# Convolution by short transforms: the last tile's slots 13-16 turned on TensorE and copied inside SBUF

## The chip, the cores and the metric

The kernel runs on one core of a Trainium2 chip. The metric is the device time in microseconds of one execution. Five engines with a queue of their own work side by side: PE (TensorE, matrix products; its weight loads are listed as PEld), DVE (VectorE), ACT (ScalarE), POOL (GpSimd) and SP (SyncE, which only issues transfers here). Each runs its instructions in the order in which they were written and waits where one of them needs something. Transfers are issued by SP or by ACT and moved by 16 DMA engines that both share. A row of the profile with SPq or ACTq is the issue of a transfer, not the transfer itself.

## The reference

```python
# x: (1, 224, 224, 96), w: (7, 7, 96, 96), both bf16
wp = jnp.pad(w, ((0, H - K), (0, W - K), (0, 0), (0, 0)))
Xf = rfft2(x, axes=(1, 2)); Wf = rfft2(wp, axes=(0, 1))      # in f32
Yf = jnp.einsum('bhwi,hwio->bhwo', Xf, Wf)
y = irfft2(Yf, s=(H, W), axes=(1, 2)).astype(jnp.bfloat16)
```

That is a circular 7x7 convolution of a 224 by 224 image with 96 channels in and 96 out.

## The kernel before

The image's 224 rows are cut into NJ = 8 blocks of B = 28 rows, and each block, with 6 rows of overlap, is taken through a short transform along the height. It has NS = 17 **slots**, each a pair of real numbers (real and imaginary part; slots 0 and 16 hold two real points each). Along the width the 7 taps are applied directly, on even and odd pixels apart. The width is cut into NT = 7 **tiles** of 32 pixels; the last is TL = 6.

A tile goes through three stages.

1. Into slots (`a_jobs`, `f_jobs`): products of image rows (tile `xn`) with the transform matrix `Fm` give `xf`, the tile's spectrum, with 96 channels on the partitions.
2. The slots (`b_round`, one call per slot). `jit` makes planes `J` of sums and differences of `xf` on DVE, for three slots at a time. Then, in PE's order: the first group of tap products into the PSUM bank `b0`, whatever `mid()` puts in, and the second group (14 products) into `b1`. ACT scales part of `b0` by -0.5 (`SE.mul`, rows `tt__NNNN<-pb`), DVE makes `u` and `v` from it (in the last tile these lie in the free `xn` buffers, so the rows say `xn<-...`), and the slot's result `yf = v + u` is summed by POOL (`ysum(GE)`) or DVE (`ysum(VE)`). In the last tile DVE takes it where `s % 3 == 2` or `s >= 14`, POOL otherwise. Where planes are made in the same round, POOL's sum waits for the last of them.
3. Back to rows (`c_jobs`). `yf` has (pixel pair, row block) on its 128 partitions; the way back needs (row block, slot, part) there. That turn goes through scratch in HBM: groups of slots are put out (`put`, `scr`, `scra`, `scrb`) and read back in the other order (`load_t`, into `tt`). Products with the matrix `G` (rows `pb<-tt,Gm`) give rows of the image, which are evicted to `yo` or `J` and written to `out`.

For tiles 0 to 5, stage 3 runs late, as filler between the slots of a later tile: `fills` and `pace` give each round of `b_round` its jobs, in `mid()` and in `end()`. Six jobs of tile 5 are left when the slots of tile 6 are done; they run behind them (`cj.pop(0)()`), and their output puts are held in `outs` until all jobs are issued.

`_Ordered` makes each engine follow the order in which its instructions are written. `evac` gives each PSUM eviction to DVE or ACT by a running sum of costs (`load`), and `tail_evac` does so behind the slots.

The last tile has no later slots to hide its way back. Its slots are split by `SLAST` = (0, 9, 12, 15, 17):

- Slots 0-8 are put to `scra` and read back by one load of 864 KB into `tl_a`, in slot 11 (`SLOAD[0]`). The products with `GA` (`first`) take these.
- Slots 9-11 and 12-14 are put to `scrb` and read back by `load_b`, into `tl_b`: the first in slot 14, the second behind the slots, on SP behind the turned copies.
- Slots 15 and 16 are turned on chip (`turn`): a product with the permutation `PT`, an eviction to `zt`, and two copies of 48 KB from SBUF to SBUF into `tl_b`, each to 8 partitions, issued on SP.

All of `tl_a` and `tl_b` lies in one `xf` buffer that is free by then (rows `xf<-scra`, `xf<-scrb`, `xf<-zt`). The products with `GB` (`second`) close the sums of `first`, wait for everything in `tl_b`, and are followed by the last evictions and eight output puts (`out_dram<-tt`). Between `first` and `second` stand WARM = 8 products without use, so that PE isn't idle.

The puts of the last tile are issued on ACT, one round late: `puts.append` in the round of a group's last slot, `puts.pop` in the next round, just behind its `SE.mul`. `YGRPL` says which slots are put together: always three, up to slots 12-14.

```python
if s in plan: ...                       # planes of the next slots: at s = 0, 3, 6, 9, 12
ydve = bool(now) if t < TL else s % 3 == 2 or s >= NS - 3
```

Of the kernel before, what the change touches and what calls it, by code (L numbers as in the profile page):

```python
# [32 lines left out]
NSLOT = 2 + 3 * (NS - 1)  # L33
PGRP = ((0, 5), (5, 8), (8, 11), (11, 14), (14, 17))
YGRP = ((0, 3), (3, 6), (6, 9), (9, 12), (12, 15), (15, 17))
YGRPL = ((0, 3), (3, 6), (6, 9), (9, 12), (12, 15), (15, 17))
SLAST = (0, 9, 12, 15, 17)
SA = SLAST[1]
ND = SLAST[-2]
SLOAD = (SA + 2, 14)  # L40
YMAX = 3
YBUF = 4
JGB = ((0, 3), (3, 6), (6, 9), (9, 12), (12, 15), (15, 17))
# [4 lines left out]
SH3 = (0, 8, 17)  # L48
MERGE = ()
NP2 = 0  # L50
WARM = 8
HEAD = ("w",) * 6 + ("x0", "w", "w", "h0", "h1", "w", "w", "x1", "w", "w")
W1 = 30
ZC = 48
# [12 lines left out]
def kernel(  # L67
# [50 lines left out]
    def bank():  # L118
        return pools["psb"].tile([128, 512], F32, name="pb")
# [30 lines left out]
    def dma(out_ap, in_ap):  # L150
        return DE.dma_start(out=out_ap, in_=in_ap)
# [455 lines left out]
    def b_round(t, s, mid, end, ydve=False, planes=()):  # L607
# [90 lines left out]
        if t == TL and s >= ND:  # L698
            turns[s] = yv.rearrange("p r m o -> p (r m o)")
        elif s == y1 - 1:  # L700
            dst, yo0 = scr_tiles[t], 0
            if t == TL:
                i = sum(s >= v for v in SLAST[1:])
                dst, yo0 = scr_tiles[(t, i)], SLAST[i]

            def put(eng=DE):
                eng.dma_start(out=dst.rearrange("w j s e -> (w j) s e")[:, y0 - yo0:y1 - yo0],
                              in_=yf[:, 0:y1 - y0].rearrange("p s r m o -> p s (r m o)"))
            if t == TL:
                puts.append(lambda: put(SE))  # L710
            else:
                put()
# [2 lines left out]
    tt_tiles = {}  # L715
    puts = []
    turns = {}

    def turn(s, copy):
        pz, i = bank()[:, 0:4 * C], s - ND  # L720
        TE.matmul(pz, lhsT=PT[:], rhs=turns[s], start=True, stop=True)
        copy(out=zt[i][:], in_=pz)
        n = 2 * (NS - ND)
        for r in range(2):
            p = RB[-1] + 2 * i + r
            dma(tl_b[p:p + (NJ - 1) * n + 1:n].rearrange("p w e -> p (w e)"), zt[i][:, r * 2 * C:(r + 1) * 2 * C])

    def load_t(t, gi, h):
        tt = t2_pool.tile([128, 12, 2 * C], BF16, name="tt2") if gi == 2 else t_pool.tile([128, 8, 2 * C], BF16, name="tt")
# [39 lines left out]
    def c_jobs(t):  # L769
        jobs = []  # L770
        w0 = t * 2 * TW
        for gi, h in LT if t < TL - 1 else LTL:
            hold = {}
            nq = 2 if gi < 2 else 3

            def mk_(q, gi=gi, h=h, nq=nq, hold=hold):
                def put(j0, nj, px, npx, row, col):
                    yo = hold["yo"]

                    def go():  # L780
                        dma(out[0, j0 * B:(j0 + nj) * B, w0 + px:w0 + px + npx, :].rearrange("h w c -> h (w c)"),
                            yo[row:row + nj * B, col:col + npx * C])
                    if tail[0] or t == TL - 1 and gi != 2:
                        outs.append(go)
                    else:
                        go()

                def f():
                    if q % 2 == 0:
                        hold["yo"] = new_yo()  # L790
                    tt = tt_tiles[(t, gi, h)]
                    yo = hold["yo"]
                    nj = 2 if q == 2 else 3
                    for b in range(2):
                        pb = bank()[0:nj * B, 0:4 * C]
                        TE.matmul(pb, lhsT=G[0:nj * FR, 0:nj * B],
                                  rhs=tt[0:nj * FR, 4 * q + 2 * b:4 * q + 2 * b + 2, :].rearrange("p w e -> p (w e)"), start=True, stop=True)
                        k = 2 * (q % 2) + b
                        evac(yo[0:nj * B, k * 4 * C:(k + 1) * 4 * C], pb, 4 * C)
                    if q == 1 and gi < 2:  # L800
                        put(gi * 3, 3, h * PXC, PXC, 0, 0)
                    elif q == 1:
                        put(6, 2, 0, 16, 0, 0)
                        for j in range(2):
                            put(6 + j, 1, 24, 8, 2 * B, j * 8 * C)
                    elif q == 2:
                        put(6, 2, 16, 8, 0, 0)
                    if q == nq - 1:
                        held[gi == 2] -= 1
                        pump()  # L810
                return f
            for q in range(nq):
                jobs.append(mk_(q))
        return jobs

    LT = ((0, 0), (1, 0), (2, 0), (0, 1), (1, 1))
    LTL = ((2, 0), (0, 0), (1, 0), (0, 1), (1, 1))
    outs = []
    NTT = 4
    held = [0, 0]  # L820
    pend = []
# [67 lines left out]
    for r in range(NS + LAG):  # L889
        if r == 0:  # L890
            for i in range(1, PGRP[0][1]):
                add(max(2 * i - 3, 0), 2 * i - 1, [diff(i)])
            for i in range(N5, REAL[1]):
                add(2 * i - (3 if i % 3 == 0 else 2), 2 * i - (i % 3 == 0), [diff(i)])
            add(0, 4, fj[1][0] + fj[1][1])
            add(8, 12, fj[2][0] + fj[2][1])
        if r == 2:
            new_xf(1, SH2[0], SH2[1])
        for p in range(3):
            if r == (1, 3, 6)[p]:  # L900
                if p:
                    new_xf(1, SH2[p], SH2[p + 1])
                else:
                    xf_tiles[1] = xf_bufs[1]
                fj = f_jobs(1, p)
                if p == 2:
                    for jg in range(2):
                        fj[jg][-1] = then_load(fj[jg][-1], 2, jg)
                add((4, 7, 12)[p], (7, 11, 15)[p], fj[0] + fj[1])
        for p in range(2):  # L910
            if r == SH3[p + 1] + 1 - p:
                new_xf(2, SH3[p], SH3[p + 1])
                fj = f_jobs(2, p)
                if p:
                    for jg in range(2):
                        fj[jg][-1] = then_load(fj[jg][-1], 3, jg)
                add(2 * r, 2 * r + (12, 5)[p], fj[0] + fj[1])
        if r == PGRP[-2][1] + 1:
            assert not any(q[2] for q in qs[:len(PGRP) - 1])
            wtmp_cm.__exit__(None, None, None)  # L920
            t_pool = ctx.enter_context(tc.tile_pool(name="tt", bufs=NTT, side="right"))
            t2_pool = ctx.enter_context(tc.tile_pool(name="tt2", bufs=1, side="right"))
            yo_pool = ctx.enter_context(tc.tile_pool(name="yo", bufs=2, side="right"))
            g_pool = ctx.enter_context(tc.tile_pool(name="gp", bufs=1, side="right"))
            GA = g_pool.tile([KA, 4 * B], BF16, name="GA")
            GB = g_pool.tile([128, 2, 4 * B], BF16, name="GB")
            GE.memset(GA[:], 0.0)
            GE.memset(GB[:], 0.0)
            PT = g_pool.tile([128, 128], BF16, name="PT")
            zt = [g_pool.tile([128, 4 * C], BF16, name=f"zt{i}") for i in range(NS - ND)]  # L930
            GE.memset(PT[:], 0.0)
            pv = PT.rearrange("p (j w) -> p j w", j=NJ)
            GE.affine_select(out=pv, in_=pv, pattern=[[-1, NJ], [-NJ, TW]], compare_op=ALU.not_equal, fill=1.0, base=0, channel_multiplier=1)
        if r == 3:
            g_fin()
        for t in range(2):
            s = r - LAG * t
            if not 0 <= s < NS:
                continue
            now = bursts.pop((r, t), ())  # L940
            now = jit(*now) if now else []
            now, rest = rest + now[:2], now[2:]
            both = LAG <= r < NS
            b_round(t, s, fills(qs, 2 * r + (t if both else 0)), fills(qs, 2 * r + (t if both else 1)), False, now)
            if r == 0:
                for d in load_x(1, 1):
                    tc.add_manual_dep(d.ins, held_x.ins.name, SYNC, reason="second half behind the first products")
# [8 lines left out]
    for t in range(2, NT):  # L956
# [22 lines left out]
        for s in range(NS):  # L979
# [10 lines left out]
            if t == TL and s in SLOAD:  # L990
                i = SLOAD.index(s)
                if i:
                    load_b(i - 1)
                else:
                    dma(tl_a.rearrange("p w g e -> p (w g) e"),
                        scr_tiles[(TL, 0)].rearrange("w (g j) s (r e) -> (j s r) (w g) e", g=2, r=2))
            b_round(t, s, fills(qs, 2 * s), fills(qs, 2 * s + 1), bool(now) if t < TL else s % 3 == 2 or s >= NS - 3, now)
    tail[0] = 1
    load["v"], load["a"] = 1000.0, 0.0
    turn(NS - 2, SE.copy)  # L1000
    for _ in range(2):
        cj.pop(0)()
    turn(NS - 1, VE.tensor_copy)
    load_b(NL - 3)
    while cj:
        cj.pop(0)()
    assert not pend
# [65 lines left out]
```

## Time and profile before

| | |
|---|---|
| runs | 263.37 us median of 3 (263.31 to 264.7) |
| profiled execution | 263.98 us; first to last instruction 262.3 us |
| PE busy | 250.6 us of the span |
| last product of slot 16 | 243.9 us |
| slot 16's sum ready | 245.16 us |
| closing products begin | 252.16 us |
| last eviction ends | 258.85 us |

Nearly every row has line L101, because all operations are recorded in the helper `_Ordered`. Rows are told apart by what they write and read: `pb` is a PSUM bank, `WF` the transformed weights, `xf`, `J`, `yf`, `zt`, `tt`, `yo` as above. Times are in microseconds from the first instruction. In a timeline, the columns are start, length, engine, line, operation, what it writes and reads, and in square brackets the idle time of the engine before it with what ended it.

### The profile page before, as it was taken

The numbers are of one execution on the slowest core, as the hardware profiler recorded it, in microseconds if no ns is written. First come the engines' busy times: TensorE is split into PE (matmuls) and PEld (weight loads), VectorE is DVE, ScalarE is ACT, GpSimd is POOL, SyncE is SP. The second block draws the span as 40 slices with busy tenths as digits, with TensorE's granted clock in tenths as the row PEclk, the third lists the DMA queues.
The fourth block names the chain that finished last, engine by engine and source line by source line (L and its number), as shares of the span: only waits on it lengthen the run. The fifth ranks groups of instructions, "written<-read, shape, count | busy, mean of one in ns | idle before, by whom it ended". The sixth has DMA issues, their size and how long they took to land.

```text
span 262.3 us, 11952 instructions
## 1 busy us (share of the span) xinstructions
PE 250.6 (96%) x5038; PEld 231.7 (88%) x5038; DVE 220.9 (84%) x463; ACT 197.4 (75%) x471; POOL 98.7 (38%) x154
## 2 busy tenths in 40 slices
PE   8999999999999999999999999999999999999873
PEld 3879999999989999989999998999999989979642
DVE  6889998899999879877887788878989799999833
ACT  8879968697745967988988789897988853564522
POOL 7782233464657532232223322334123422325000
PEclk9999999999999999999999999999999999999987
DMA  7995104511111698987985495949949942788984
GB/s 182 268 185 134 47 6 143 169 51 47 47 49 50 189 267 145 322 251 195 265 232 190 139 280 165 229 115 300 278 164 214 296 143 82 201 215 223 201 272 151
DMA packets 46766, 46.58 MB, mean 178 GB/s; under 512 B 35312, under 2 KB 37940, under 8 KB 46712
## 3 DMA queue, kind: packets, MB, share of 16 engines
q1 hardware_dynamic: 45992, 44.34, 61.4%
q10 hardware_dynamic: 720, 1.47, 1.7%
q8 instruction: 39, 0.64, 1.0%
q14 instruction: 15, 0.12, 0.2%
HBM read 24.46 MB, written 21.14 MB: 174 GB/s over the span
## 4 chain that ended last, share of the span: by engine, by line
PE 68%; DVE 12%; DMA 9%; issue 4%; ACT 3%; POOL 2%; SPq 1%; DVEq 0%; POOLq 0%; ACTq 0%
PE pb L101 66%; DVE J L101 4%; DMA tt<-scr 3%; DMA WF<-in_x_dram 3%; DVE xn L101 2%; DVE WF L101 2%; DVE yf L101 2%; DMA wq<-in_w_dram 2%; POOL yf L101 2%; SPq L101 1%; DMA xf<-scrb 1%; ACT xf L101 1%; DVE v L101 1%; PE ps L101 1%; ACT WF L101 1%
## 5 line engine op out<-in xcount | busy, mean ns | idle before, releaser
L101 PE MATMUL pb<-WF,J 96*128 96x96 bf16 x2821 | 162.4, 206 | 1.6 <-DVE J L101 0.8
L101 PEld LDWEIGHTS <-J 96*128 96x128 bf16 x2821 | 138.0, 98 | 10.6 <-issue 3.5
L101 POOL TENSOR_TENSOR yf<-v,u 128x384 bf16<-128x384 f32 x70 | 73.0, 1056 | 124.0 <-issue 72.5
L101 ACT CAST xf<-pb 96x408 bf16<-96x408 f32 (+6 forms) x140 | 65.0, 492 | 3.6 <-PE pb L101 1.4
L101 PE MATMUL pb<-WF,xf 96*128 96x96 bf16 x952 | 59.9, 206 | 0.2
L101 DVE TENSOR_TENSOR J<-xf 96x456 bf16<-96x456 bf16 (+3 forms) x85 | 56.3, 701 | 0.0
L101 PEld LDWEIGHTS <-xf 96*128 96x128 bf16 x952 | 47.2, 98 | 1.0 <-PE ps L101 0.6
L101 PE MATMUL pb<-Fm,xn 118*128 118x136 bf16 (+4 forms) x576 | 43.8, 203 | 0.3 <-ACT xf L101 0.3
L101 PE MATMUL pb<-tt,Gm 102*84 102x384 bf16 (+1 forms) x132 | 32.1, 326 | 0.5 <-DMA tt<-scr 0.4
L101 ACT CAST yo<-pb 84x384 bf16<-84x384 f32 (+1 forms) x61 | 26.2, 482 | 5.5 <-PE pb L101 4.3
L101 PEld LDWEIGHTS <-xn 118*128 118x128 bf16 x576 | 28.7, 97 | 0.5 <-issue 0.4
L101 ACT CAST J<-pb 84x384 bf16<-84x384 f32 (+1 forms) x64 | 27.5, 490 | 0.0
L101 DVE TENSOR_TENSOR J<-J 96x912 bf16<-96x912 bf16 (+2 forms) x42 | 25.3, 603 | 0.0
L101 ACT CAST WF<-pb 96x480 bf16<-96x480 f32 x42 | 21.3, 566 | 0.1
L101 PEld LDWEIGHTS <-wq 128*128 128x128 bf16 (+1 forms) x288 | 19.6, 148 | 1.0 <-issue 1.0
L101 PE MATMUL pb<-wq 128*128 128x120 bf16 x192 | 15.2, 224 | 0.0
L101 DVE TENSOR_TENSOR WF<-WF 96x960 bf16<-96x960 bf16 x15 | 14.0, 932 | 1.4 <-ACT WF L101 1.3
L101 POOL TENSOR_TENSOR yf<-xn,xn 128x384 bf16<-128x384 f32 x9 | 8.8, 998 | 14.8 <-issue 12.1
L101 PEld LDWEIGHTS <-Gm 102*84 102x84 bf16 (+1 forms) x132 | 11.4, 117 | 1.8 <-DMA tt<-scr 0.6
L101 DVE TENSOR_TENSOR yf<-v,u 128x384 bf16<-128x384 f32 x20 | 11.6, 578 | 0.7
L101 ACT COPY xf<-xf 96x816 bf16<-96x816 bf16 (+4 forms) x18 | 10.8, 659 | 0.0
L101 DVE CAST tt<-pb 112x384 bf16<-112x384 f32 x8 | 4.2, 556 | 5.9 <-PE pb L101 5.8
(405 smaller groups left out, 267.5 us busy)
## 6 DMA issues: line engine op xcount, KB each, us to landing
scr<-yf SPq DMA_DIRECT2D x30, 288.0 KB
xn<-in_x_dram SPq DMA_DIRECT2D x12, 672.0 KB
tt<-scr SPq DMA_DIRECT2D x24, 336.0 KB
out_dram<-yo SPq DMA_DIRECT2D x12, 252.0 KB
out_dram<-J SPq DMA_DIRECT2D x12, 252.0 KB
tt<-scr SPq DMA_DIRECT2D x6, 288.0 KB
wq<-in_w_dram SPq DMA_DIRECT2D x5, 288.0 KB
WF<-in_x_dram SPq DMA_DIRECT2D x2, 672.0 KB
```

The lines of the kernel that those rows point to most:

```text
L101: r = fn(*a, **k)
```

## The change

- The last tile's slots are split by `SLAST` = (0, 9, 13, 17). Slots 9-12 form one reload of 384 KB; slots 13-16 are all turned on chip, which makes eight copies of 48 KB instead of four. The second reload of 288 KB is gone, and so is the scratch for it.
- The last tile's groups are (9, 11), (11, 13), (13, 15), (15, 17) behind slot 9. Slots 9, 10 are put on ACT in slot 11. Slots 11, 12 are put on SP at the end of slot 12 itself.
- The reload of slots 0-8 moves from slot 11 to slot 13, behind that put on SP, and is split into two transfers (48 and 24 partitions). The reload of 9-12 stays in slot 14.
- The turn is cut in two functions. Slots 13 and 14 are turned inside slots 15 and 16: `turned` adds the product, the ACT eviction and two SP copies to `mid()`. Slots 15 and 16 are turned behind the slots; the copies of 15 are issued on SP, those of 16 on ACT.
- `zt` lies in the first four slots of `WF`, which are no longer needed.
- Behind the slots, one late job of tile 5 runs as before. The evictions of the next two are held in `waiting` and written behind those of the turned slots.
- WARM goes from 8 to 4. With fewer groups, `g_parts` makes 20 small copies of `G` instead of 28.

```diff
-YGRPL = ((0, 3), (3, 6), (6, 9), (9, 12), (12, 15), (15, 17))
-SLAST = (0, 9, 12, 15, 17)
+YGRPL = ((0, 3), (3, 6), (6, 9), (9, 11), (11, 13), (13, 15), (15, 17))
+SLAST = (0, 9, 13, 17)
-SLOAD = (SA + 2, 14)
+SLOAD = (13, 14)
-WARM = 8
+WARM = 4
...
-            if t == TL:
+            if t == TL and s < SLAST[2] - 1:
                 puts.append(lambda: put(SE))
             else:
                 put()
...
+    zt = [WF[:, i].rearrange("p t o -> p (t o)")[:, 0:4 * C] for i in range(NS - ND)]
+    laid, loads_a = [], []
+
+    def turn_mm(s):
+        pz = bank()[:, 0:4 * C]
         TE.matmul(pz, lhsT=PT[:], rhs=turns[s], start=True, stop=True)
-        copy(out=zt[i][:], in_=pz)
-        n = 2 * (NS - ND)
+        return pz
+
+    def turn_out(s, pz, copy, eng):
+        i, n = s - ND, 2 * (NS - ND)
+        copy(out=zt[i], in_=pz)
         for r in range(2):
             p = RB[-1] + 2 * i + r
-            dma(tl_b[p:p + (NJ - 1) * n + 1:n].rearrange("p w e -> p (w e)"), zt[i][:, r * 2 * C:(r + 1) * 2 * C])
+            d = eng.dma_start(out=tl_b[p:p + (NJ - 1) * n + 1:n].rearrange("p w e -> p (w e)"), in_=zt[i][:, r * 2 * C:(r + 1) * 2 * C])
...
+    def turned(mid, s):
+        def f():
+            mid()
+            turn_out(s, turn_mm(s), SE.copy, DE)
+        return f
...
-                        evac(yo[0:nj * B, k * 4 * C:(k + 1) * 4 * C], pb, 4 * C)
+                        ev = (yo[0:nj * B, k * 4 * C:(k + 1) * 4 * C], pb, 4 * C)
+                        if tail[0] == 2:
+                            waiting.append(ev)
+                        else:
+                            evac(*ev)
...
-                    dma(tl_a.rearrange("p w g e -> p (w g) e"),
-                        scr_tiles[(TL, 0)].rearrange("w (g j) s (r e) -> (j s r) (w g) e", g=2, r=2))
-            b_round(t, s, fills(qs, 2 * s), fills(qs, 2 * s + 1), bool(now) if t < TL else s % 3 == 2 or s >= NS - 3, now)
+                    sv = scr_tiles[(TL, 0)].rearrange("w (g j) s (r e) -> (j s r) (w g) e", g=2, r=2)
+                    for p0, p1 in ((0, 48), (48, KA)):
+                        loads_a.append(dma(tl_a[p0:p1].rearrange("p w g e -> p (w g) e"), sv[p0:p1]))
+            mid = fills(qs, 2 * s)
+            if t == TL and s - 2 in turns:
+                mid = turned(mid, s - 2)
+            b_round(t, s, mid, fills(qs, 2 * s + 1), bool(now) if t < TL else s % 3 == 2 or s >= NS - 3, now)
...
-    turn(NS - 2, SE.copy)
+    cj.pop(0)()
+    tail[0] = 2
     for _ in range(2):
         cj.pop(0)()
-    turn(NS - 1, VE.tensor_copy)
-    load_b(NL - 3)
+    tail[0] = 1
+    pz = [turn_mm(s) for s in (NS - 2, NS - 1)]
+    turn_out(NS - 2, pz[0], VE.tensor_copy, DE)
+    turn_out(NS - 1, pz[1], SE.copy, SE)
+    load["v"], load["a"] = 0.0, 700.0
+    for ev in waiting:
+        evac(*ev)
     while cj:
         cj.pop(0)()
```

More of the change, by code (lines that the diff above doesn't have):

```diff
@@ L717 @@
     turns = {}
-    def turn(s, copy):
-        pz, i = bank()[:, 0:4 * C], s - ND
+    zt = [WF[:, i].rearrange("p t o -> p (t o)")[:, 0:4 * C] for i in range(NS - ND)]
+    laid, loads_a = [], []
+    def turn_mm(s):
+        pz = bank()[:, 0:4 * C]
         TE.matmul(pz, lhsT=PT[:], rhs=turns[s], start=True, stop=True)
-        copy(out=zt[i][:], in_=pz)
-        n = 2 * (NS - ND)
+        return pz
+    def turn_out(s, pz, copy, eng):
+        i, n = s - ND, 2 * (NS - ND)
+        copy(out=zt[i], in_=pz)
         for r in range(2):
             p = RB[-1] + 2 * i + r
-            dma(tl_b[p:p + (NJ - 1) * n + 1:n].rearrange("p w e -> p (w e)"), zt[i][:, r * 2 * C:(r + 1) * 2 * C])
+            d = eng.dma_start(out=tl_b[p:p + (NJ - 1) * n + 1:n].rearrange("p w e -> p (w e)"), in_=zt[i][:, r * 2 * C:(r + 1) * 2 * C])
+            for q in loads_a:
+                tc.declare_no_dep(d.ins, q.ins, reason="other columns of the tile")
+            if laid and eng is SE:
+                tc.add_manual_dep(d.ins, laid[-1].ins.name, NOSYNC, reason="order of transfers")
+            laid.append(d)
+    def turned(mid, s):
[3 more added lines that the diff above has]
+        return f
     def load_t(t, gi, h):
@@ L818 @@
     outs = []
+    waiting = []
     NTT = 4
@@ L929 @@
             PT = g_pool.tile([128, 128], BF16, name="PT")
-            zt = [g_pool.tile([128, 4 * C], BF16, name=f"zt{i}") for i in range(NS - ND)]
             GE.memset(PT[:], 0.0)
```

## The prediction

> **What bounds the kernel now.** The page comes first: its head, and the shares of the chain that ended last.
>
> ```profile
> span 262.3 us, 11952 instructions
> PE 250.6 (96%) x5038; PEld 231.7 (88%) x5038; DVE 220.9 (84%) x463; ACT 197.4 (75%) x471; POOL 98.7 (38%) x154
> PE 68%; DVE 12%; DMA 9%; issue 4%; ACT 3%; POOL 2%; SPq 1%; DVEq 0%; POOLq 0%; ACTq 0%
> ```
>
> Over the whole run TensorE (PE) is the bound. The diff touches only the last tile, though, so the price is read in the last 25 us. There the chain in order of time (start, length, what) says:
>
> ```profile
> 244.13 0.57 DVE yf L101
> ...
> 248.68 3.44 DMA xf<-scrb
> 252.12 0.04 issue
> 252.16 5.64 PE pb L101 x22
> ```
>
> VectorE (DVE) carries the end of the slots. Then everything waits for the reload of slots 12-14, and the closing products start at 252.16. This is the timeline of the SP queue, with all reloads and turned copies of the last tile:
>
> ```profile
> 238.44 0.31 SPq L101 DMA_DIRECT2D xf<-scra  x1
> 244.94 0.33 SPq L101 DMA_DIRECT2D xf<-scrb  x1
> 245.70 2.88 SPq L101 DMA_DIRECT2D xf<-zt  x4
> 248.68 0.41 SPq L101 DMA_DIRECT2D xf<-scrb  x1
> ```
>
> A turned copy costs SP 0.69 us to issue (2.88 over 4 with their gaps). Next the timelines of ScalarE (ACT) and of POOL around slot 11:
>
> ```profile
> 236.50 0.41 ACT L101 ACTIVATE tt__7115<-pb 128x288 f32<-128x288 f32 x1
> 237.21 0.85 ACT L101 CAST yo<-pb 84x384 bf16<-84x384 f32 x2 [0.30 <-PE pb L101]
> 238.23 0.41 ACT L101 ACTIVATE tt__7162<-pb 128x288 f32<-128x288 f32 x1 [0.17 <-ACT yo L101]
> 239.13 0.33 ACTq L101 DMA_DIRECT2D scrb<-yf  x1
> ```
>
> ```profile
> 236.68 1.96 POOL L101 TENSOR_TENSOR yf<-xn,xn 128x384 bf16<-128x384 f32 x2 [3.15 <-issue]
> 241.00 1.96 POOL L101 TENSOR_TENSOR yf<-xn,xn 128x384 bf16<-128x384 f32 x2 [2.35 <-issue]
> ```
>
> The ACT rows are the scaling of slot 11, two late evictions, the scaling of slot 12, and the put of slots 9-11, which waited for slot 11's sum. The POOL rows are the sums of slots 9, 10 and of 12, 13: slot 10 is ready at 238.64, slot 12 at 242.0, slot 13 at 242.96. Last the busy times by stretch (PE, PEld, DVE, ACT, POOL, granted clock, DMA share, GB/s):
>
> ```profile
> 240.00:245.00 5.00, 4.05 (x93) 3.88 (x90) 4.93 (x12) 1.20 (x4) 1.96 (x2) 1.00 0.97 227
> 243.30:246.72 3.42, 2.47 (x26) 1.81 (x24) 2.69 (x7) 1.84 (x6) 0.00 (x0) 1.00 0.94 244
> 250.13:253.54 3.41, 1.65 (x10) 0.98 (x9) 0.97 (x2) 0.81 (x3) 0.00 (x0) 1.00 0.91 312
> 253.54:256.95 3.41, 3.41 (x12) 2.27 (x11) 1.73 (x4) 1.44 (x5) 0.00 (x0) 0.50 0.78 255
> ```
>
> DVE has no slack before the end of the slots (4.93 of 5.00), the transfers are full (0.97), and the clock is halved for 3.41 us inside the closing products, after a stretch in which PE was busy only 1.65 of 3.41.
>
> **The change part by part.** All sums are against the profiled execution: 263.98 us, of which 262.3 is the span. The median of the runs is 263.37, which is 0.61 lower, so I subtract 0.61 at the end.
>
> *The put of slots 9, 10.* Puts on ACT are popped just behind the scaling of the next slot. Before, that slot was always a multiple of three, and the sum it waited for was a quick one on DVE. Now slots 9, 10 are put behind slot 11's scaling (done 236.91), but slot 10's sum is a POOL sum, ready at 238.64. ACT stands until about 239.03 (0.33 for the issue). Behind it on ACT are the two evictions (0.85, to 239.95) and slot 12's scaling (0.41, to 240.35 instead of 238.64). DVE's next operation needs that scaling: 240.4 instead of 238.98, **1.4 late**. DVE has nothing to give it back with, so the planes of the last slots end at 242.3 instead of 240.86, and POOL's sum of slot 12, which waits for them, at 243.4 instead of 242.0; slot 13 at 244.4.
>
> *Turning slots 13, 14 inside slots 15, 16.* It adds two products (0.33 each), two ACT copies (0.48) and four SP issues (2.8). The product for slot 13 stands in PE's order inside slot 15, which PE reaches at about 242.9 (242.25 before, plus 0.65 for the late planes). It waits for slot 13's sum until 244.4. Queued behind are slot 15's last 14 products, on which DVE waits: they end at 245.3, and DVE's operation on them starts 1.8 later than 243.56. One more sum (0.56), slot 16's 22 products and the turn of 14 (1.35) follow; slot 16's sum ends at about 247.25 instead of 245.16, **2.1 late**.
>
> *The puts and reloads on SP.* The put of slots 11, 12 stands ahead of the big reload (864 KB) and waits for slot 12's sum: 243.45. The big reload, now two issues, leaves at 243.8 instead of 238.44, **5.4 later**. The reload of 9-12 (384 KB) waits for the landing of that put. SP then issues six copies (4.2) and the held output puts. No other transfer was waiting on SP between 237.2 and 243.4, so that stretch itself costs nothing.
>
> *The transfers.* In 384-byte packets, before: 2304 + 768 + 768 loaded and 512 copied. After: 2304 + 1024 loaded, 1024 copied. The sum is the same, 4352; what goes is a wait for an HBM round trip in the middle, and what comes is the late start. Three answers on packets of the SP queue (packets, MB, share), in 240.4-242.4, 248-250.2 and 227-227.6:
>
> ```profile
> q1 hardware_dynamic: 955, 0.37, 91.7%
> ```
>
> ```profile
> q1 hardware_dynamic: 684, 0.25, 55.8%
> ```
>
> ```profile
> q1 hardware_dynamic: 484, 0.19, 110.7%
> ```
>
> So the big load itself ran at 480 a us beside a put, and a full-width load at 807. I take 580, nearest to the row of the same load now without a put beside it: 3328 packets, 5.7 us (4.1 to 6.9). The copies ran at 311 a us or more, being issue-limited; at full share that row would be 557. I take 420 between them: 2.4 (1.8 to 3.3). The first packet came about 0.75 after the issue (238.44, packets from 239.2); the put's 128 packets take 0.6 (0.07 us each, eight to an engine, as for the outputs at the end: 313 packets in 1.5 us at 0.9). Sum: 243.45 + 0.75 + 0.6 + 5.7 + 2.4 = 252.9, and 0.3 for the landing: **closing products at 253.2** instead of 252.16 (bounds 251.6, by SP's issues, and 255.6).
>
> *Two queues for slots 15, 16.* ACT's two issues (1.4) spare SP as much; the packets stay in the same pile. They hold ACT's evictions to 249.7, and five evictions at 0.42 end at 251.8; the eight first products, which need those banks, at 252.2, and four warming products at 252.85. That is hidden by the transfers, but only by 0.35 us. Eight fewer small copies of the G matrix and the smaller number of warming products lie under this wait or two tiles earlier, and cost nothing.
>
> *The closing products.* Before they took 6.7 (252.16 to the last eviction at 258.85), 3.41 of it at half clock. PE would now idle some 0.4 to 1 us instead of 1.76. A stretch busy at 2.47 of 3.42 was not followed by half clock, one at 1.65 was; 2.4 to 3.0 is nearer the first, so I take full clock: 24 products at 0.163 and 16 evictions on two engines (0.55 and 0.48) make about 4.8, to 258.0. Now the transfers bound the end: 252.9, the held outputs 3.2 (336 packets of 3 KB, 251.2 to 254.4 before), the last outputs 4.4, the landing 0.6: 261.1, against 261.28 before. **Net -0.2**: 263.8 profiled, 263.2 for the median; I say 263.3.
>
> [...]
>
> [...]
>
> **Rivals.**
>
> *Half clock stays.* If PE's idle falls in one window with its sparse work before, the closing products take 6.7 again: 253.2 + 6.7 = 259.9 against 258.85, +1.05, **264.4**. For it: the share of 250.13-253.54, and PE's late evictions; against it: the shorter idle.
>
> *Copies at half width.* If the copies use no more engines than in 248-250.2, they run at that row's 311 a us: 3.3 us instead of 2.4, and what ends the kernel comes 0.9 later, **264.2**. For it: the share of 55.8% with little else in flight; against it: SP's slow issue explains that share as well.
>
> *SP held by the landing (slower).* The reload of 9-12 and all copies stand behind the landing of the put of 11, 12. Before, the put at 239.13 released SP only at 244.94, 5.8 later. If this put takes as long, SP goes on at 249.25, issues for 4.5 to 253.8, and the last copy lands near 255.5; with half clock 255.5 + 6.7 = 262.2, +3.3. At 4.5 us it is +2.0. I say **265.8**. It decides from about 3.9 us. Against it: this put is ahead of the load on its own queue.
>
> *Faster.* Transfers at the upper rates, a quick landing, full clock: closing products at 251.6, the outputs follow without a gap, the end 2.0 earlier: **261.5**. For it: full-width rates were seen.
>
> **How the numbers follow.** Forecast 0.30, half clock 0.15, half width 0.12, SP held 0.23, faster 0.20. A measurement tells about 0.5% (1.3 us) from no change. Slower (over 264.7): all of SP held, a third of half clock and a quarter of half width, 0.31. Faster (under 262.05): the fast case, and as much from below the forecast as it gives up itself, 0.20. Within: 0.49. The range 261.5 to 265.8 reaches to the middle of both outer cases and leaves out 0.2; the forecast's own range is 262.3 to 264.3.
>
> **What would show it.** Right: an ACT gap of about 2 us before the put at 238.7, the big reload near 243.8, a PE wait for slot 13's sum inside slot 15, PE's last wait on a copy ending near 253, clock 1.00 behind it. Wrong: slot 16's sum at 245-246, an SP wait over 4 us on the put, or a half-clock stretch.

## The result, and the profile after

The changed kernel takes 273.54 us (median of 6 runs, 273.21 to 276.56) against 263.12 us (6 runs, 261.86 to 264.7) for the kernel before: a ratio of 1.041 (95% interval 1.036 to 1.047). The forecast was 263.3 with a range of 261.5 to 265.8, so the time lies 7.7 us beyond its slow end. The profiled execution of after took 273.55 us.

The page of after, its head and the shares of the chain that ended last:

```profile
span 271.8 us, 11947 instructions
PE 252.2 (93%) x5036; PEld 232.1 (85%) x5036; DVE 221.6 (82%) x463; ACT 198.5 (73%) x473; POOL 98.6 (36%) x154
PE 68%; DVE 10%; DMA 10%; issue 4%; ACT 3%; POOL 2%; SPq 1%; ACTq 0%; DVEq 0%; POOLq 0%
```

The engines do nearly the same work as before: PE is busy for 252.2 us against 250.6, DVE for 221.6 against 220.9. The span grew by 9.5 us, so it is mostly waiting that came. The chain of after in order of time says where:

```profile
242.98 2.57 DMA scrb<-yf
245.55 0.02 issue
245.57 2.24 SPq L101
...
247.91 9.52 DMA xf<-WF
257.43 0.02 issue
257.45 0.61 ACTq L101
258.06 0.04 issue
258.10 0.48 ACT J L101
258.58 0.04 issue
258.63 5.84 PE pb L101 x18
```

The put of slots 11, 12 lands (2.57). SP sends the reload of 9-12. The first copy of slot 13 is issued at 247.91 and lands only 9.52 later. Then comes something that no step of the prediction has: ACT issues a copy (`ACTq`) when *another* slot's copy has landed, and does a late eviction behind it (`ACT J`), for which PE stood. The timeline of SP, the issues of the last tile's loads and copies:

```profile
242.98 0.35 SPq L101 DMA_DIRECT2D scrb<-yf  x1
243.38 1.89 SPq L101 DMA_DIRECT2D xf<-scra  x2
245.57 2.24 SPq L101 DMA_DIRECT2D xf<-scrb  x1
247.91 7.50 SPq L101 DMA_DIRECT2D xf<-WF  x6
```

The big load leaves at 243.38 (238.44 before), in two parts. The reload took 2.24 us to issue, and the six copies 7.50, 1.25 each where the four of before took 2.88, 0.72 each: SP itself is held while it issues. The timelines of ACT, POOL and PE:

```profile
236.19 0.41 ACT L101 ACTIVATE tt__7104<-pb 128x288 f32<-128x288 f32 x1
238.37 0.33 ACTq L101 DMA_DIRECT2D scrb<-yf  x1
...
247.32 0.48 ACT L101 CAST WF<-pb 128x384 bf16<-128x384 f32 x1 [0.29 <-PE pb L101]
255.10 2.96 ACTq L101 DMA_DIRECT2D xf<-WF  x2
258.10 1.23 ACT L101 CAST J<-pb 84x384 bf16<-84x384 f32 x3 [10.30 <-DMA xf<-WF]
```

```profile
236.38 1.96 POOL L101 TENSOR_TENSOR yf<-xn,xn 128x384 bf16<-128x384 f32 x2 [3.15 <-issue]
241.96 1.95 POOL L101 TENSOR_TENSOR yf<-xn,xn 128x384 bf16<-128x384 f32 x2 [3.62 <-DVE J L101]
```

```profile
255.16 1.18 PE L101 MATMUL pb<-xf,GA 72*112 72x384 bf16 x3 [6.14 <-DMA xf<-scra]
258.63 2.00 PE L101 MATMUL pb<-xf,GA 72*112 72x384 bf16 x5 [2.29 <-ACT J L101]
260.42 1.48 PE L101 MATMUL pb<-wu 128*112 128x384 bf16 x4
261.70 0.52 PE L101 MATMUL pb<-xf,GB 128*112 128x384 bf16 x1
```

ACT stood at the put of slots 9, 10 until POOL's sum of slot 10 (238.37), and stood again for 10.30 us with the two copies of slot 16. PE's first products waited 6.14 us for the big load, the next five for ACT's late evictions, and the closing products began at 261.70 instead of 252.16. Busy times by stretch (PE, PEld, DVE, ACT, POOL, granted clock, DMA share, GB/s):

```profile
240.00:245.00 5.00, 3.26 (x71) 2.94 (x68) 4.64 (x12) 1.50 (x4) 1.95 (x2) 1.00 0.13 44
250.31:253.73 3.42, 0.00 (x0) 0.00 (x0) 0.00 (x0) 0.00 (x0) 0.00 (x0) 0.50 1.34 95
260.55:263.97 3.42, 3.42 (x13) 2.24 (x12) 1.12 (x2) 1.23 (x3) 0.00 (x0) 0.50 0.43 152
263.97:267.40 3.43, 2.95 (x18) 2.08 (x16) 2.93 (x6) 2.40 (x6) 0.00 (x0) 1.00 0.76 222
```

Between 240 and 245 the transfers are nearly idle (0.13; 0.97 before). In 250.31-253.73 no engine does anything, while the transfers are more than full by their records (1.34) and move 95 GB/s. The clock is 1.00 again only behind 263.97. The packets of the SP queue (packets, MB, share of 16 engines) in 246-252 and in 252-255 say how slow they were:

```profile
q1 hardware_dynamic: 2134, 0.81, 137.3%
```

```profile
q1 hardware_dynamic: 803, 0.30, 114.7%
```

That is 356 and 268 packets a us. The share times 16 engines times the window, divided by the packets, is the mean time that one took: 1.373 x 16 x 6 / 2134 = 62 ns, then 69 ns. The row of before in 240.4-242.4 gives 31 ns for packets of the same 384 bytes.

### The profile page after: what moved, and what is told of

Read it like the earlier page. It is cut to its first block, busy times and chain, and to the rows that moved or that the text cites. A ratio compares the mean times of both kernels' runs of the same rounds, so it can differ in the third digit from the quotient of the medians.

```text
span 271.8 us, 11947 instructions
## 1 busy us (share of the span) xinstructions
PE 252.2 (93%) x5036; PEld 232.1 (85%) x5036; DVE 221.6 (82%) x463; ACT 198.5 (73%) x473; POOL 98.6 (36%) x154
## 4 chain that ended last, share of the span: by engine, by line
PE 68%; DVE 10%; DMA 10%; issue 4%; ACT 3%; POOL 2%; SPq 1%; ACTq 0%; DVEq 0%; POOLq 0%
PE pb L101 68%; DVE J L101 4%; DMA xf<-WF 4%; DVE WF L101 3%; DMA WF<-in_x_dram 3%; POOL yf L101 2%; DMA wq<-in_w_dram 2%; DVE v L101 1%; ACT xf L101 1%; SPq L101 1%; DMA scrb<-yf 1%; DMA out_dram<-tt 1%; ACT WF L101 1%; DVE xn L101 1%; DVE u L101 1%
## 5 line engine op out<-in xcount | busy, mean ns | idle before, releaser
L101 ACT CAST J<-pb 84x384 bf16<-84x384 f32 (+1 forms) x64 | 27.6, 489 | 10.5 <-DMA xf<-WF 10.3
L101 ACT CAST WF<-pb 96x480 bf16<-96x480 f32 (+1 forms) x45 | 22.5, 554 | 1.8 <-PE pb L101 1.7
L101 PE MATMUL pb<-xf,GA 72*112 72x384 bf16 x16 | 6.0, 426 | 8.4 <-DMA xf<-scra 6.1
```

The lines of the kernel that those rows point to most:

```text
L101: r = fn(*a, **k)
```

## The experiments

Four theories were set against each other. *Rows*: the 384-byte packets themselves take longer than predicted, more so in the two-part load. *Marks*: transfers wait for each other although their data don't, and ACT with them. *Landing*: SP is held by the landing of the put of 11, 12. *Start*: the load leaves 5 us late. All ratios are to the kernel before, run beside each; its median was 263.04 to 263.75 us in these sessions, so a difference of some tenths between two versions' times says little.

The profiled executions already differ ahead of the part that the edits move: POOL's sum of slot 10 ends between 237.70 and 239.60. Where starts of closing products are compared between runs, they are therefore also counted from the end of that sum (238.64 in before, 238.34 in after). A table behind the experiments has most of them.

**The load in one part; the load cut by columns.** In after, the two parts of 48 and 24 partitions become one load of 72, or two of all 72 partitions and half the pixel pairs each.

```diff
-                    for p0, p1 in ((0, 48), (48, KA)):
+                    for p0, p1 in ((0, KA),):
```

> The changed kernel, with the big reload (slots 0-8) again as one transfer to 72 partitions instead of 48 and 24. [...] Rival 'late' (the reload is slow because of when it runs, whatever its cut): no change, 273.5.

> The changed kernel, with the big reload still in two transfers, but cut by columns, each to all 72 rows. [...] Rival 'two transfers' (any second transfer costs it): 273.5 as before.

271.17 us (ratio 1.030, 1.026 to 1.033) and 271.76 (1.030, 1.025 to 1.036). Both give back about 2 us, so the cut by rows costs it, not the second transfer as such. Packets of the one load in 246-252:

```profile
q1 hardware_dynamic: 2206, 0.84, 114.4%
```

50 ns each, against 62; those of the two column parts took 46 (2404 packets at 115.7%). The same edit made in the other direction, on the kernel before:

> The kernel before, with its big reload in two parts of 48 and 24 rows, at its old place in slot 11, and nothing else changed. Theory 'rows': the reload lands 3 to 4 us later than 246.75, the reloads and copies behind it on the same queue follow, and the closing products start 2 to 3 us later: 265 to 266. Rival 'late': no change, 263.1 within 0.5.

264.21 (1.004, 1.001 to 1.008): 1 us, less than the expected 2 to 3, although the packets in 240-242 take 63 ns:

```profile
q1 hardware_dynamic: 688, 0.26, 136.4%
```

The parts landed at 244.50 and 246.50, the one load of before at 246.75. Counted from slot 10's sum, that is 8.4 us against 8.1: packets of twice the time made the landing only 0.3 us later.

**The copies of slot 16 on SP.** `turn_out(NS - 1, pz[1], SE.copy, DE)`, to free ACT.

> The changed kernel, with slot 16's two copies issued on SP like the others instead of on ACT. Theory 'marks' (a transfer is not issued until the earlier one that signals on the same semaphore has landed; here that holds the issue of 16's copies until 255.0 and 257.4, and on ACT it also holds the late evictions from 247.8 to 258.1): SP is held just as long, the copies land as late, near 260.8, but the evictions and the first products are through before; the closing products begin near 261 instead of 261.7, the kernel ends 0.5 to 2 us earlier, 271.5 to 273. Rival 'ACT alone' (the held evictions are the whole loss): back to 263 to 265.

273.46 (1.038, 1.035 to 1.042): nothing. ACT's wait was gone and its evictions were done at 249.53, but the eight first products only moved to where the load let them, and the eighth copy left SP at 256.42:

```profile
247.75 9.27 SPq L101 DMA_DIRECT2D xf<-WF  x8
254.76 2.78 PE L101 MATMUL pb<-xf,GA 72*112 72x384 bf16 x8 [6.22 <-DMA xf<-scra]
260.14 1.82 PE L101 MATMUL pb<-xf,GB 128*112 128x384 bf16 x5 [1.31 <-DMA out_dram<-J]
```

(The last row names an output, but by the landings PE waited there for the eighth copy, which landed at 259.79.) The closing products began 1.56 earlier, yet half clock until 265.66 (263.98 in after) took that back. So marks hold ACT for 10.3 us, but that is not what costs the 10 us of the result. Where ACT's wait comes from is seen in the order of instructions, where every transfer waits for the completion mark, of eight taken in turn, of the transfer eight before it (190 and 192 stand on SP, 364 and 365 on ACT; `DMAHW4` and `DMAHW6` are two of the marks):

```
190 L101 DMACopy xf_68<-scra 24x32x192 [waits DMAHW4_49]
192 L101 DMACopy xf_68<-WF 8x16x192 [waits DMAHW6_49,Activation_49]
...
364 L101 DMACopy xf_68<-WF 8x16x192 [waits DMAHW4_49,Activation_49]
365 L101 DMACopy xf_68<-WF 8x16x192 [waits DMAHW6_49]
```

In the trace of after, too, the 218 issues use eight marks, and none begins before the last transfer with its mark has landed; the closest begins 16 ns behind. ACT's two copies of slot 16 come eight transfers behind the second part of the big load, which landed at 255.02 (ACT's issue: 255.10), and behind slot 13's first copy, which landed at 257.43 (257.45).

**The put of slots 9, 10 on SP.** It undoes step one of the prediction, ACT's wait for POOL: `if t == TL and s < SA:`.

> The changed kernel, with slots 9 and 10 put on SP at the end of slot 10 instead of on ACT in slot 11. Theory 'hold' (the ACT put waits for POOL's sum of slot 10 and holds evictions, scaling and DVE behind it, 1.2 us): DVE's idle 1.18 before slot 12 goes, POOL's sum of slot 12 ends near 241.8 instead of 242.95, the big reload leaves 1.1 to 1.3 earlier and the kernel ends as much earlier, 272.2 to 272.5. Rival: the hold is covered by something else that is late, and the end does not move, 273.5.

272.04 (1.033, 1.026 to 1.041): 1.5 us by the medians. The put of 11, 12 left at 241.49 instead of 242.98.

**Only the load's start, on before.** `SLOAD = (13, 14)` in the kernel before.

> The kernel before, with its big reload in one transfer issued in slot 13 instead of slot 11, and nothing else changed. It leaves SP 2 to 3 us later (238.4 before). Theory 'late': the reloads and copies behind it start as much later, and the kernel ends 2 to 3 us later, near 265.5, with the packets themselves slow. Theory 'rows': the packets keep 22 to 38 ns; the end moves by no more than the start, 0 to 2.5 us, 263 to 265.5.

263.15 (0.999, 0.996 to 1.002), and the load left at 238.87, as always. The expectation was wrong, and so this tests nothing of *start*: SP is tied to no slot, only to what stands ahead in its queue, here the landing of the put of 6-8 at 238.85.

**The load ahead of the put of 11, 12.** `SLOAD = (11, 14)` in after.

> The changed kernel, with the big reload (still in two parts) written on SP ahead of the put of slots 11 and 12 instead of behind it. Theory 'order on SP' (the reload is late only because SP holds it behind a put that waits for slot 12's sum): it leaves near 238.2 instead of 243.4, lands by 247.5, and the rest follows 4 to 6 us earlier; closing products near 256, kernel 266 to 269. Rival 'pile' (the transfers are as slow as they are because of the turned copies and the reload of 9-12, whenever they start): the gain is under 3 us, 270.5 to 273. By theory 'marks' slot 16's first copy then waits on the put of 11, 12 instead of the reload, and leaves before 250.

270.37 (1.025, 1.019 to 1.032): 3.2 us of the expected 4.5 to 7.5. The load now left at 238.16, but *landing* appeared: the put, behind the load's packets, took from 243.06 to 248.65, and the reload of 9-12 left right then.

```profile
243.06 0.34 SPq L101 DMA_DIRECT2D scrb<-yf  x1
248.66 0.58 SPq L101 DMA_DIRECT2D xf<-scrb  x1
```

*Marks* is borne out here: slot 16's first copy now came eight transfers behind that put and was issued on ACT at 248.72, just after the put had landed. The second one again waited for slot 13's first copy (254.27), and PE's next five products waited for ACT's evictions:

```profile
255.46 2.00 PE L101 MATMUL pb<-xf,GA 72*112 72x384 bf16 x5 [4.98 <-ACT J L101]
```

**All of these at once.** One load, ahead; puts of 9-12 on SP; all copies on SP.

> The changed kernel with what the other runs accuse taken back at once, and the turning of slots 13-16 kept: the big reload in one transfer and ahead of the put of 11, 12; the puts of 9, 10 and of 11, 12 both on SP; slot 16's copies on SP. If late start, row parts and the hold on ACT are the loss: reload lands near 247, the reload of 9-12 near 250, copies until 253.5, and the kernel takes 263 to 265.5. Rival 'copies' (eight small copies inside SBUF are the slow part themselves): 267 or more.

269.38 (1.022, 1.016 to 1.029), not 263 to 265.5. The put of 11, 12 landed at 248.23, eight copies left SP from 248.96 to 254.2 (0.65 each), and closing products began at 256.59.

**The reload behind the copies.** The last kernel and after (there `(13, 14)` becomes `(13,)`), each with the reload of 9-12 behind the copies of 13-16, so that none of these stands behind that landing.

```diff
-SLOAD = (11, 14)
+SLOAD = (11,)
     turn_out(NS - 1, pz[1], SE.copy, DE)
+    load_b(0)
```

> The run before this with one load ahead of slot 11, all last puts and all copies on SP (269.38, closing products at about 256.6), but with the reload of slots 9 to 12 written behind the eight turned copies. So no copy stands behind the landing of the put of 11, 12 any more. 'SP held by the landing' (the rival of the prediction): the copies leave from about 245.5, as soon as each slot is turned; SP is through with them by about 250.5, the reload follows, and all has landed near 253.5; 266 to 267. 'Rows' (384-byte packets are slow whatever the order): the pile takes as long as before, 268.5 to 270.

> The changed kernel with one thing turned round: the reload of slots 9 to 12 is written behind the copies of slots 13 to 16, so that no copy stands behind the landing of the put of 11, 12 on SP. 'SP held by the landing' alone: the landing held SP until 245.57, and in the run with one load taken back as well this order gave 2.5 us, so 271 to 272. 'Pile': the same packets are in flight from 243 to 260 in another order, so that the reload is last instead of the copies: 272.5 to 274.5.

266.83 (1.013, 1.008 to 1.018) for the first, 2.5 us less by the medians, as *landing* expects. But the two intervals overlap, and in the profiled executions the closing products, counted from slot 10's sum, began only 0.4 us earlier (16.56 against 16.99); so what the landing cost there is not settled. On after itself, where the put lands within 2.8 us, the same order gives 0.8 by the medians: 272.76 (1.035, 1.028 to 1.041). There the reload is last instead, landing at 258.60, with ACT's second copy at 258.83 (260.80 in after). The closing products began 2.5 us earlier, at 259.18 (2.2 by the count from slot 10's sum; the row names an output, but the eighth copy had landed just before, at 258.83):

```profile
259.18 1.82 PE L101 MATMUL pb<-xf,GB 128*112 128x384 bf16 x5 [0.92 <-DMA out_dram<-J]
```

Half clock lasted to 265.33, and from their start to the last eviction they took 7.84 us instead of 5.96. So the order did matter to the transfers of after; the clock took most of it back.

**Two thirds of the load early.** The load of slots 0-8 is cut by slots instead of by rows. Slots 0-5 get a scratch of their own, are loaded in slot 9 and take partitions 0-47; slots 6-8 stay where the load stood. The small copies of G follow. This goes into after, into the last kernel ("both"), and into before.

```diff
+            if t == TL and s == EARLY:          # EARLY = 9
+                load_a("e", 0, 8 * SE6)         # slots 0 to 5, SE6 = 6
...
-                    for p0, p1 in ((0, 48), (48, KA)):
-                        loads_a.append(dma(tl_a[p0:p1].rearrange("p w g e -> p (w g) e"), sv[p0:p1]))
+                    load_a(0, 8 * SE6, KA)
```

> The changed kernel, with the load of slots 0 to 8 cut by slots: 0 to 5 leave in slot 9, while the last products with tile 5 are still under way, and 6 to 8 in slot 13, behind the put of 11, 12. The row cut is gone with it. If the transfers behind 243 are the cost, as the trace after says, 1536 of 3328 loaded packets are out of their way: the last copy lands 4 to 6 us earlier than 260.8, and the kernel takes 267.5 to 269.5. If it is the chain of put, landing, reload of 9 to 12 and eight copies on SP, it takes no less than the one load ahead of slot 11 did: 269.4 to 270.4.

> Turned copies ahead of the reload of 9 to 12, all on SP, and slots 0 to 5 loaded early: both of the accused together. If packets and the landing are all that was left, the closing products begin at 251.5 to 252.5, as in the kernel before or a little sooner, and it takes 262.5 to 264.5. If the longer slots (DVE 1.4 and slot 16's sum 2 us late) and eight issues at 0.6 on SP count by themselves, it stays at 265 to 267.

> The kernel before, with the load of slots 0 to 8 cut by slots: 0 to 5 (1536 of its 2304 packets) leave in slot 9, near 233.5, and 6 to 8 where the whole load stood, in slot 11. The scratch and the small copies of G follow. If the pile of 384-byte packets between 239 and 252 sets when the closing products can begin, the puts of 9 to 11 and 12 to 14 land sooner (2.5 us each instead of 5), the last reload leaves near 246.5 to 248 and the products begin 1 to 2.5 us earlier: 260.8 to 262.3. If the chain of slot 14's sum, put, landing and reload sets it by itself, or the earlier packets only hold up tile 5's transfers, no change: 262.9 to 264.

After with the early part: **266.09 (1.011, 1.006 to 1.016)**, 7.4 of the 10.4 us back with one edit, more than the row cut's 2.4, which is undone in it too, and more than expected. Its packets in 246-252, and its issues:

```profile
q1 hardware_dynamic: 1694, 0.63, 54.0%
```

```profile
236.79 0.37 SPq L102 DMA_DIRECT2D xf<-scre  x1
242.49 0.35 SPq L102 DMA_DIRECT2D scrb<-yf  x1
242.89 0.39 SPq L102 DMA_DIRECT2D xf<-scra  x1
246.49 0.59 SPq L102 DMA_DIRECT2D xf<-scrb  x1
247.17 4.03 SPq L102 DMA_DIRECT2D xf<-WF  x6
```

31 ns a packet instead of 62, and SP isn't held any more: 0.59 for the reload, 0.67 a copy. Both together: 266.80 (1.013, 1.008 to 1.018), no better than either alone. Its closing products began earlier than in both, 15.99 us behind slot 10's sum against 16.56 and 17.59, but half clock covered 6.35 us of them, and they took 7.94 us to the last eviction (7.00 and 6.14):

```profile
253.69 1.85 PE L102 MATMUL pb<-xf,GB 128*112 128x384 bf16 x5 [4.52 <-DMA xf<-scrb]
```

```profile
253.54:256.95 3.41, 3.26 (x11) 2.23 (x12) 1.67 (x3) 1.43 (x4) 0.00 (x0) 0.50 0.66 232
256.95:260.37 3.42, 3.42 (x13) 2.40 (x12) 1.43 (x3) 1.34 (x3) 0.00 (x0) 0.55 0.48 143
```

Before with the early part: 264.16 (1.001, 0.997 to 1.005), no change; the last reload left at 248.58 (248.68 before) and landed at 252.09 (252.12). This run decides little: the early part left SP only at 236.53 instead of near 233.5 and landed at 244.26, and the rest of the load landed at 246.61 (246.75 before), so the pile was hardly lighter.

**The order once more.** In "both", the reload of 9-12 was last, 248.47 to 253.65. It was put between the copies of 14 and 15; and likewise, in before with the early part, the reload of 12-14 between the copies of 15 and 16.

> The last run with everything together (266.8), with the reload of slots 9 to 12 written ahead of the copies of slots 15, 16 instead of behind all eight. In that run the put of 11, 12 had landed at 246.41 and the eight copies at 249.96, but the reload, written last, left at 248.47 and landed at 253.65. If the order on SP's queue is what is left of the loss, the reload leaves near 246.5 and lands near 251, the copies of 15, 16 leave by 249.5 and land by 251.5, and the closing products begin at 251 to 252: 263.5 to 265. If the reload takes its 5 us wherever it stands, because its packets share the engines with the copies and the outputs, they begin near 253 as before: 266 to 267.

> The kernel before with slots 0 to 5 loaded early (264.16, ratio 1.001), and with the reload of slots 12 to 14 ahead of the two copies of slot 16 instead of behind them. In that run the put of 12 to 14 had landed at 247.50, but the reload left at 248.58 and landed at 252.09, last of all. If the same reading holds there, it leaves at 247.6, lands near 251, and the closing products begin about 1 us sooner: 262 to 263.2. If the copies, now 0.4 later each, take its place, no change: 263 to 264.5.

265.75 (1.008, 1.004 to 1.013) and 264.49 (1.002, 0.998 to 1.006). In the first, the put of 11, 12 landed only at 248.33, so the reload left then and not at 246.5, and the copies of 15, 16 became the last to land (254.71). In the second, the reload landed at 251.95, slot 16's copies at 252.39, and the closing products began at 252.53, no earlier than before (252.16). In both, another transfer took the last place and landed as late as the former last or later. No version beat the kernel before.

The profiled executions side by side (us). The second column of numbers is the start of the closing products behind the end of slot 10's sum, the third is the time from there to the last eviction, which is long where half clock covers it.

| | median of the runs | closing products begin | to the last eviction |
|---|---|---|---|
| before | 263.12 | 13.52 | 6.69 |
| after | 273.54 | 23.36 | 5.96 |
| after, load in one part | 271.17 | 21.32 | 6.74 |
| after, copies of slot 16 on SP | 273.46 | 21.96 | 7.53 |
| after, put of 9, 10 on SP | 272.04 | 21.67 | 5.95 |
| after, load ahead of the put | 270.37 | 20.13 | 5.27 |
| after, reload behind the copies | 272.76 | 21.21 | 7.84 |
| all of these at once | 269.38 | 16.99 | 6.85 |
| the same, reload behind the copies | 266.83 | 16.56 | 7.00 |
| after, early part | 266.09 | 17.59 | 6.14 |
| both together | 266.80 | 15.99 | 7.94 |
| both, reload between the copies | 265.75 | 16.47 | 7.26 |

## Why the prediction was wrong

*The put of slots 9, 10: right.* ACT stood from 236.60 to 238.37 for the sum of slot 10. Slot 12's sum ended 4.61 us behind slot 10's instead of 3.36, 1.25 late where 1.4 was predicted. In the five runs with this put on SP it is 3.35 or 3.36 again, and the run that moves only this put is 1.5 us shorter.

*Turning 13, 14: right, a little less.* PE's product for slot 13 started at 243.96 after 1.32 us of waiting (244.4 predicted). Slot 16's sum ended at 246.64, 1.5 late instead of 2.1 (1.8 counted from slot 10's sum, and 0.5 where the put of 9, 10 is on SP).

*The puts and reloads on SP: right to the issue.* The put left at 242.98, the load at 243.38 (243.45 and 243.8 predicted). The put landed in 2.57, below the 3.9 from which the slower rival, SP held by the landing, was to decide. Even so the copies behind that landing came later than they had to: with the reload behind them, the last landing came 1.6 us earlier, counted from the put. Where the load was sent ahead of the put, the put landed 5.3 to 6.9 us behind slot 12's sum, which it waits for (2.6 in after).

*The transfers: the step that failed.* It gave 0.75 + 0.6 + 5.7 + 2.4 us from the put to the last copy, 252.9; the last copy landed at 260.80. The order of the terms was right and their size wrong: 17.8 us instead of 9.45. The prediction took rates from the best stretches of 2 us or less (580 and 420 packets a us) and called them those of the whole pile. It also read the copies' rate from a row that does not hold copies alone: 684 packets in 248-250.2, where the copies have 512 in all and the reload of 9-11 landed at 249.45. The trace of before already had the whole: 4538 packets of the SP queue between 239.2 and 252.1 are 352 a us with SP's own waits in it, and the big load alone ran from 238.44 to 246.75, 8.3 us. From that row 3328 + 1024 packets take 12.4 us, which ends near 257.2. The remaining 3.6 were new. Of the 17.8 us from the put to the last copy, undoing the row cut takes 2.0, issuing slot 16's copies on SP instead of ACT 0.9, and the reload behind the copies 1.6; each was tried alone, and they need not add. (A smaller slip: 2.88 us over four copies are 0.72 each, not 0.69.)

Whether the 16 engines carried the pile evenly is not shown by any run. The traces show completions: in after, the load's part of 48 partitions and the reload of 64 report 16 each; the part of 24 reports 12 and each turned copy 8, besides one mark just behind the issue. The whole load of 72 in before reports 12 as well.

*Two queues: failed too.* ACT's evictions were to be done at 251.8, hidden by 0.35. ACT stood until 258.10, since its copies waited for the marks of earlier transfers. The diff puts two more issues on ACT, and the prediction counted their time, not their waits. By itself that wait cost nothing that the time shows (copies on SP: 273.46): without it the closing products began 1.56 earlier, and the longer half clock took that back.

*The closing products: wrong in the clock, small.* Half clock held from 250.33 to 263.98; PE had been busy for 1.81 us in 246.90-250.31 and for nothing in 250.31-253.73. From their start to the last eviction they took 5.96 us (6.7 before, 4.8 predicted). Of the rivals, half clock came true in part; the copies at half width were the nearest idea to what happened, 0.9 us where 8 were needed.

*What the 10.4 us are.* Most of it is the load of slots 0-8 running in 243 to 255, on the path, instead of 238 to 247, under the slots: 7.4 us come back when most of it leaves early, the row cut's share among them, and 3.2 when it only starts ahead of the put, since then the put's landing takes its place. These gains overlap and don't add. Some 2.7 to 3.6 us remain in the four best versions with slots 13-16 turned. There the last transfer of the pile lands at 253.65 to 255.34, against 252.12 in before, and in three of them half clock lasts 6.83 us instead of 3.41. By the table, their closing products begin 2.5 to 4.1 us later than in before and take between 0.6 less and 1.3 more. Where the put of 9, 10 is on SP, the slots end only 0.5 later than in before by the same count, so longer slots explain no more than that. How the rest splits between eight issues of 0.6 us and the reload stays open.

## What to carry to other kernels

Price a pile of small packets from its issue to its last landing in the trace, in the same mix, and not from its busiest two microseconds (580 and 420 packets a us were taken here, the whole pile of before ran at 352). Price a transfer that used to run under other work and is moved behind a wait as time on the path, and look at what is in flight with it: here 7.4 of the 10.4 us came back when two thirds of the load left early, and a packet in 246-252 took 31 ns instead of 62. Before an issue is put on an engine that also computes, look which earlier transfer it has to wait for, data or no data (here ACT stood for 10.3 us). When two versions are compared, look where the part in question begins in each trace, and not only at the total: here the clock took back several gains.

## What the runs showed that was not expected

- Cutting a load of 72 partitions at row 48 made its 384-byte packets slower, 62 ns against 50 in after and 63 against 29 in before (240-242, where before has 980 packets at 87.5%). Two parts by columns did not cost that (46 ns). The cut by rows also changes the completions: 16 and 12 for the parts in after, 12 for the whole load in before. Why the packets were slower is not shown.
- Issuing a transfer itself took long: 2.24 us for the reload and 1.25 us a copy on SP in after, while packets took 62 ns; 0.59 and 0.67 with the early part, where they took 31.
- A copy on ACT's queue held ACT for 10.3 us on transfers whose data it did not need.
- An earlier start of the closing products did not always make an earlier end. With slot 16's copies on SP they began 1.56 us earlier and with the reload behind the copies 2.5, for 0.1 and 0.8 us of time, since half clock (to 265.66 and 265.33 instead of 263.98) covered more of them.
